# A gated linear attention and two dense blocks on one core: state products in four quarters of the array, y in two banks

## The chip, the cores and the metric

The kernel runs on one core of a Trainium2 chip. The metric is the device time of one execution in microseconds (us); the time before is the median of three runs, 859.57 us (857.78 to 859.61). The engines are TensorE (PE, with its weight loads as PEld), VectorE (DVE), ScalarE (ACT), GpSimd (POOL) and SyncE (SP), which issues nearly all transfers.

## The reference

Three parts follow one another, all in float32.

```python
for t in range(S):                                   # B, H, S, D = 4, 8, 768, 48
    state = alpha[:, :, t, :, None] * state + einsum('bhd,bhe->bhde', k[:, :, t], v[:, :, t])
    y[:, :, t] = einsum('bhd,bhde->bhe', q[:, :, t], state)
x = y as (B * S, H * D)                              # 3072 tokens, 384 columns
h = x @ w_in; x = (max(h, 0) + alpha * min(h, 0)) @ w_out      # 384 -> 2048 -> 384
return ((x @ w1) * (x @ w2)) @ w3 @ w_out2                     # 384 -> 1024 -> 1024 -> 384
```

## The kernel before

The attention is computed in 24 chunks of 128 time steps, six to each of the four batches; chunk n belongs to batch n // 6. Within a chunk the gates are multiplied up along time by a scan on VectorE, so that the recurrence becomes a masked product of scores with v, plus q times the state that the chunk starts from. The eight heads are laid out as four pairs: pair p holds its two heads (hh = 0 and 1) in partitions 0 to 47 and 64 to 111 of the tiles of q and k, and v is padded to 64 columns for each head.

The function `chunk` (line 340) traces the TensorE work of one chunk in this order: `state` (line 277) computes the update of the state, eight products into the tile `Up`; `yout` (line 293) computes y; `scores` (line 261) computes the scores of the next chunk into two tiles `scp`. `yout` has two stages that add into one PSUM bank `yp` of 128 x 512: eight products of v with the masked scores (`yp<-sc,v`), and eight of the state with q (`yp<-qt,sst`). A chunk that begins a batch (n % 6 == 0, `alone`) has no second stage. Head hh of pair p writes partitions 64 hh to 64 hh + 63 and column block p of the bank. So in the first stage the two heads of a pair use all 128 rows of the array and either its left or its right 64 columns; in the second stage head 0 uses rows 0 to 63 and columns 0 to 63, head 1 rows 64 to 127 and columns 64 to 127. The trace shows every one of these float32 products as two records, so a stage of eight products is 16 records of TensorE and 16 weight loads.

After its products, y is copied from the bank by ScalarE (line 310 for chunks 2 and 3, line 315 for the others; the helper `copy` is line 72), and `place` (line 321) moves it one tick later into the operand tile of the first dense block by six transfers for each copied piece, whole pairs 0 to 2 first and then pair 3 in four pieces (`PIECES`) that fill the remaining 32 partitions of each of the three column groups. The rows of `w_in` are put in the same order on the host.

The dense blocks work on 512 tokens at a time (T = 0 to 5), with `w_in` and `w_out` in high and low parts (`three`). `G1(T, f)` (line 377) makes nine products into a bank of 128 x 512 of the pool `pab` (tag `h`, two buffers that are taken in turn); ScalarE reads it (`u`, line 384) and then VectorE (`g`, line 386), after which the bank is free. `G2(T, f)` (line 391) makes nine products into three accumulators of the pool `pacc`, whose other three banks, by the parity w of T, are used by `Up`, `yp`, `scp` and `kTp` of the attention (`bank`, line 107). The eight PSUM banks are these six and the two of `pab`. The main loop goes through the pairs (T, f); each turn traces G1, some units of the attention, G2 of two turns earlier, and some units again (`attend`, line 465). Within a chunk the products made by `mm` (line 236) are pinned to their traced order on TensorE; elsewhere a planner orders the instructions of PE, DVE, ACT and POOL by costs of its own, and SP keeps the traced order.

In the opening (lines 407 to 446) four chunks run before any dense product, with dense products of a tile of zeros (`warm_up`, line 426) in between that also take the banks of `pab` in turn. After the attention, from about 430 us, TensorE works on the dense blocks alone. A fallback for gates outside a range of values (line 635 on) is in the program and isn't run on these inputs.

Of the kernel before, what the change touches and what calls it, by code (L numbers as in the profile page):

```python
# [9 lines left out]
F32 = mybir.dt.float32  # L10
# [11 lines left out]
B, H, S, D = 4, 8, 768, 48  # L22
DM, DFF, DF2 = 384, 2048, 1024
NT = B * S
CH = 128
NC_B = S // CH
NSTEP = B * NC_B
NP = H // 2
KD = DM // 128
DP = 64  # L30
# [19 lines left out]
def pieces():  # L50
    out, j = [], 0
    while j < 2 * D:
        (hh, e), (k, i) = divmod(j, D), divmod(j, EXT)
        n = min(D - e, EXT - i)
        out.append((k, 2 * D + i, hh, e, n))
        j += n
    return out


PIECES = pieces()  # L60
# [3 lines left out]
def fused_kernel(ctx, tc, qk, al, vv, wf, ws, m_alpha, ident, maskn, out):  # L64
# [3 lines left out]
    def f32(ap):  # L68
        return ap.bitcast(F32)

    def copy(out, in_):
        act.activation(out=out, in_=in_, func=AF.Copy)  # L72
# [7 lines left out]
    pab = ctx.enter_context(tc.tile_pool(name="pab", bufs=2, space=PSUM))  # L80
# [26 lines left out]
    def bank(shape, name, which):  # L107
        i = turn[which]
        turn[which] = (i + 1) % KD
        return pacc.tile(shape, F32, tag=f"acc{i}_{which}", name=name)  # L110
# [7 lines left out]
    sst = [ap1.tile([128, NP, DP], F32, name=f"sst{i}") for i in range(2)]  # L118
# [4 lines left out]
    def later(k, fn):  # L123
        due.setdefault(clock[0] + k, []).append(fn)
# [111 lines left out]
    def mm(*a, **k):  # L236
        ins = pe.matmul(*a, **k)  # L237
        if tight[0]:
            tc.keep_in_program_order(ins)
        tight[0] = True  # L240
# [34 lines left out]
    pairs = [(p, hh, slice(64 * hh, 64 * hh + DP)) for p in range(NP) for hh in range(2)]  # L275
# [17 lines left out]
    def yout(n, w):  # L293
        qt, v = st.pop(("qt", n)), st.pop(("v", n))
        sc = [st.pop(("sc", n, hh)) for hh in range(2)]
        alone = n % NC_B == 0
        ps = bank([128, NP, CH], "yp", w)
        for p, hh, r in pairs:
            mm(ps[r, p], v[:, 2 * p + hh], sc[hh][:, p], start=p == 0, stop=alone and p == NP - 1,
                      skip_group_check=True)  # L300
        if not alone:
            for p, hh, r in pairs:
                mm(ps[r, p], sst[n % 2][r, p], qt[r, p], start=False, stop=p == NP - 1, skip_group_check=True)
        T, c = divmod(n, SPT)
        if c == 0:
            new_x(T)
        single = n in (2, 3)
        if single:
            y = gp.tile([128, NP, CH], F32, tag="x1", name="yT1", bufs=KD)
            copy(y, ps)  # L310
        else:
            if c % 2 == 0:
                st["yT"] = ap2.tile([128, NP, 2, CH], F32, tag="yT", name="yT", bufs=1)
            y = st["yT"]
            copy(y[:, :, c % 2], ps)
            if c % 2 == 0:
                return
            y = y.rearrange("p a c t -> p a (c t)")
        x = f32(xt[T][:, 1, :, (c if single else c - 1) * CH:(c + 1) * CH])

        def place():
            q = (sp, act) if n == SPT - 1 else (sp, sp)
            for hh in range(2):
                q[hh].dma_start(out=x[hh * D:(hh + 1) * D], in_=y[64 * hh:64 * hh + D, :KD])
            for i, (k, to, hh, e, n_) in enumerate(PIECES):
                q[i % 2].dma_start(out=x[to:to + n_, k], in_=y[64 * hh + e:64 * hh + e + n_, KD])

        later(1, place)
# [3 lines left out]
    def new_x(T):  # L332
        xt[T] = xp.tile([128, 2, KD, TA], F32R, tag="x", name="x")
# [6 lines left out]
    def chunk(n, w, more=True):  # L340
        untie()
        state(n, w)
        yout(n, w)
        if more:
            scores(n + 1, w)
        load_v(n + 3)
# [60 lines left out]
    with tc.manual_schedule(engines={mybir.EngineType.SP}):  # L407
# [65 lines left out]
        for g in range(NG + LAG):  # L473
# [47 lines left out]
            if g in spans:  # L521
                U, steps = spans[g]
                pend = attn_units(U)
                tot, used, half = len(pend), 0, 0
# [22 lines left out]
        for i in range(NJ):  # L547
            t = w3_s[i]
            ps = bank([128, DM], "w34", 0)
# [86 lines left out]
    with tc.If(bad > 0):  # L636
        with tc.tile_pool(name="fa", bufs=1) as fa:
            S_ = fa.tile([128, NP, D], F32, name="S_")
            blk = fa.tile([128, 2], F32, name="blk")
            dve.memset(blk, 0.0)  # L640
            for hh in range(2):
                dve.memset(blk[64 * hh:64 * hh + 64, hh:hh + 1], 1.0)
            with tc.For_i(0, B, 1) as b:
                dve.memset(S_, 0.0)
                with tc.For_i(0, NC_B, 1) as c:
                    one = (bass.ds(b, 1), bass.ds(c, 1))
                    at = fa.tile([128, NP, CH], F32, name="at")
                    qt = fa.tile([128, 2, NP, CH], F32, name="qt")
                    vt = fa.tile([128, H, DP], F32, name="vt")
                    sp.dma_start(out=at, in_=al[one].rearrange("b c p a t -> p (b c a) t"))  # L650
                    sp.dma_start(out=qt, in_=qk[one].rearrange("b c p i a t -> p (b c i) a t"))
                    sp.dma_start(out=vt, in_=vv[one].rearrange("b c s h e -> s (b c h) e"))
                    for g in range(CH // TG):
                        yt = fa.tile([2, TG, NP, D], F32, name="yt")
                        for i in range(TG):
                            t = g * TG + i

                            def col(ap):
                                return ap[:, :, t:t + 1].to_broadcast([128, NP, D])

                            sel = fa.tile([128, 128], F32, name="sel")
                            dve.tensor_copy(out=sel, in_=idn[:, t:t + 1].to_broadcast([128, 128]))
                            vb = pacc.tile([128, NP, 2, D], F32, tag="acc0_0", name="vb")
                            pe.matmul(vb.rearrange("p a i e -> p (a i) e"), sel, vt[:, :, :D], start=True, stop=True)
                            kv = fa.tile([128, NP, D], F32, name="kv")
                            for hh in range(2):
                                r = slice(64 * hh, 64 * hh + 64)
                                dve.tensor_tensor(out=kv[r], in0=vb[r, :, hh],
                                                  in1=qt[r, 1, :, t:t + 1].to_broadcast([64, NP, D]), op=ALU.mult)
                            dve.tensor_tensor(out=S_, in0=S_, in1=col(at), op=ALU.mult)  # L670
                            dve.tensor_tensor(out=S_, in0=S_, in1=kv, op=ALU.add)
                            z = fa.tile([128, NP, D], F32, name="z")
                            dve.tensor_tensor(out=z, in0=S_, in1=col(qt[:, 0]), op=ALU.mult)
                            yp = pacc.tile([2, NP * D], F32, tag="acc1_0", name="yp")
                            pe.matmul(yp, blk, z.rearrange("p a e -> p (a e)"), start=True, stop=True)
                            copy(yt[:, i].rearrange("p a e -> p (a e)"), yp)
                        dst = y_d[one][:, :, g * TG:(g + 1) * TG]
                        whole = [(k, hh * D, hh, 0, D, k) for k in range(KD) for hh in range(2)]
                        for k, to, hh, e, n_, a in whole + [piece + (KD,) for piece in PIECES]:
                            sp.dma_start(out=dst[:, :, :, k, to:to + n_].rearrange("b c t e -> (b c) t e"),  # L680
                                         in_=yt[hh:hh + 1, :, a, e:e + n_])

        with tc.tile_pool(name="fb", bufs=1) as fb:
            wi = fb.tile([128, NF, KD, 128], F32, name="wi")
# [5 lines left out]
            for f in range(NF):  # L690
                for o, dst in enumerate((wi[:, f].rearrange("p k f -> p (k f)"), wo[:, f])):
                    t = fb.tile([128, DM, 2], I32, name="rw")
                    sp.dma_start(out=t.bitcast(I16).rearrange("p n c -> p (n c)")[:, :4 * DM - 1],
                                 in_=wf[f, :, o].bitcast(I16)[:, 1:])
                    upper(zf, t)
                    assemble(dst.bitcast(I32), zf, t)
            with tc.For_i(0, NTA, 1) as T:
                x = fb.tile([128, KD, TA], F32, name="xf")
                yv = y_d.rearrange("b c t k e -> (b c t) (k e)")
                for c in range(SPT):  # L700
                    yr = fb.tile([128, DM], F32, name="yr")
                    sp.dma_start(out=yr, in_=yv[bass.ds(T * TA + c * CH, CH)])
                    for k in range(KD):
                        ps = bank([128, 128], "tp", 1)
# [3 lines left out]
                for f in range(NF):  # L708
                    ps = pab.tile([128, TA], F32, tag="h", name="h")
                    for k in range(KD):  # L710
                        pe.matmul(ps, wi[:, f, k], x[:, k], start=k == 0, stop=k == KD - 1)
                    g = gp.tile([128, TA], F32, tag="g", name="g")
# [10 lines left out]
        with tc.tile_pool(name="fx", bufs=2) as fx:  # L723
            with tc.For_i(0, NTA, 1) as T:
                y = fx.tile([128, KD, TA], F32, name="x1")
                sp.dma_start(out=y, in_=x1_d[bass.ds(T, 1)].rearrange("b p k t -> p (b k) t"))
                e = xp.tile([128, 2, KD, TA], F32R, tag="x", name="x")
# [52 lines left out]
```

## Time and profile before

| | |
|---|---|
| median of three runs | 859.57 us (857.78 to 859.61) |
| the profiled execution | 856.45 us, span 854.7 us |
| PE busy | 834.7 us, 98% of the span, 4772 records |
| PEld busy | 686.0 us, 80% |
| DVE busy | 459.5 us, 54% |
| ACT busy | 352.6 us, 41% |
| POOL busy | 11.1 us, 1% |
| state products `yp<-qt,sst`, whole span | 320 records, 21.8 us busy, mean 275 ns |
| products with the scores `yp<-sc,v`, whole span | 384 records, 25.4 us busy, mean 275 ns |

The span runs from the first to the last recorded instruction of the profiled execution; its own time is 1.75 us longer. Busy time of an engine counts overlapping instructions once. A record of a TensorE product lasts longer than the step to the next one, since the products go through the array one behind the other and their ends are modelled. A merged row of the timeline reaches from the first start to the last end. L237 is the line of the helper `mm`, so the stages of a chunk are told apart by their tiles.

### The profile page before, as it was taken

What the parts mean: (1) busy time and instruction counts of PE and PEld (TensorE: products, weight loads), DVE (VectorE), ACT (ScalarE), POOL (GpSimd) and SP (SyncE); (2) the same over time, 40 slices, a digit from 0 to 9 for tenths busy, and PEclk for the clock granted to TensorE, in tenths of its full rate; (3) what the DMA queues carried; (4) which work ended last, traced back from release to release, by engine and by line L of the source; (5) the groups of instructions that cost most, each with busy time, mean ns of one, the idle gap of its engine ahead of it and who ended that gap; (6) DMA issues with size and microseconds to landing.
All of it is one profiled execution on the core that took longest, in us unless ns stands there. A gap on an engine that the chain in (4) does not pass through costs nothing.

```text
span 854.7 us, 11911 instructions
## 1 busy us (share of the span) xinstructions
PE 834.7 (98%) x4772; PEld 686.0 (80%) x4776; DVE 459.5 (54%) x643; ACT 352.6 (41%) x538; POOL 11.1 (1%) x53
## 2 busy tenths in 40 slices
PE   7899999999999999999999999999999999999996
PEld 4577888888888888888888889988888888888884
DVE  7899876665685586656335634552434435322221
ACT  3567665434454545454335534522223232221221
POOL 0000000000000000000000000000000000000000
PEclk9999999999999999999999999999999999999998
DMA  7667572321673385525003306420302203010001
GB/s 279 221 202 248 181 257 97 105 79 39 227 254 106 129 297 184 184 108 196 3 18 111 123 1 224 141 79 1 134 14 74 74 25 124 1 38 1 37 1 41
DMA packets 49104, 99.56 MB, mean 116 GB/s; under 512 B 4880, under 2 KB 25488, under 8 KB 49040
## 3 DMA queue, kind: packets, MB, share of 16 engines
q1 hardware_dynamic: 48800, 98.62, 34.0%
q8 instruction: 39, 0.64, 0.3%
q14 instruction: 25, 0.20, 0.1%
q10 hardware_dynamic: 240, 0.10, 0.0%
HBM read 75.63 MB, written 18.35 MB: 110 GB/s over the span
## 4 chain that ended last, share of the span: by engine, by line
PE 91%; DVE 4%; ACT 2%; issue 1%; DMA 1%; ACTq 0%; DVEq 0%; SPq 0%
PE ab L372 23%; PE h L372 21%; PE acc L372 11%; PE acc L397 8%; PE acc L398 7%; PE acc L400 7%; PE yp L237 4%; PE w L372 4%; PE scp L237 2%; PE Up L237 1%; PE kTp L256 1%; DMA al<-in_al_dram 1%; DVE al L214 1%; DVE w L151 1%; DVE sc L272 1%
## 5 line engine op out<-in xcount | busy, mean ns | idle before, releaser
L372 PE MATMUL h<-x,w 128*128 128x512 f32 x864 | 213.8, 391 | 3.5 <-ACT x L72 3.0
L372 PE MATMUL ab<-x,w 128*128 128x512 f32 x864 | 203.6, 389 | 0.0
L372 PEld LDWEIGHTS h<-x,w 128*128 128x128 f32 x864 | 161.3, 188 | 37.9 <-ACT x L72 3.5
L372 PEld LDWEIGHTS ab<-x,w 128*128 128x128 f32 x864 | 162.1, 188 | 33.6
L397 PE MATMUL acc<-gs,w 128*128 128x512 f32 x288 | 115.4, 401 | 0.0
L398 PE MATMUL acc<-gs,w 128*128 128x512 f32 x288 | 113.1, 393 | 0.0
L576 DVE TENSOR_TENSOR c<-ab,a 128x512 f32<-128x512 f32 x48 | 33.1, 690 | 145.3 <-PE ab L372 145.3
L384 ACT ACTIVATE u<-h,sgn 128x512 f32<-128x512 f32 x96 | 65.5, 682 | 108.0 <-PE h L372 107.8
L386 DVE SCALAR_TENSOR_TENSOR g<-h,salpha,u 128x512 f32<-128x512 f32 x96 | 71.7, 747 | 68.1 <-ACT u L384 67.7
L372 PE MATMUL acc<-cs,w 128*128 128x512 f32 x432 | 105.8, 389 | 0.0
L389 DVE SCALAR_TENSOR_TENSOR gs<-g,sgn,gs 128x512 fp32r<-128x512 f32 x96 | 71.9, 749 | 51.1 <-ACT gs L388 51.0
L372 PEld LDWEIGHTS acc<-cs,w 128*128 128x128 f32 x432 | 81.0, 188 | 17.2 <-DVE cs L579 0.4
L388 ACT ACTIVATE gs<-g,sgn 128x512 fp32r<-128x512 f32 x96 | 69.1, 719 | 54.0 <-DVE g L386 54.0
L400 PE MATMUL acc<-gs,w 128*128 128x512 f32 x288 | 81.4, 391 | 0.0
L72 ACT ACTIVATE a<-ab 128x512 f32<-128x512 f32 x48 | 28.8, 599 | 109.9 <-PE ab L372 109.9
L72 ACT ACTIVATE cs<-c 128x512 fp32r<-128x512 f32 x48 | 30.2, 629 | 93.4 <-DVE c L576 93.4
L397 PEld LDWEIGHTS acc<-gs,w 128*128 128x128 f32 x288 | 54.4, 189 | 12.4 <-issue 0.2
L400 PEld LDWEIGHTS acc<-gs,w 128*128 128x128 f32 x288 | 54.5, 189 | 11.6
L398 PEld LDWEIGHTS acc<-gs,w 128*128 128x128 f32 x288 | 54.5, 189 | 10.7
L72 ACT ACTIVATE top<-raw 128x768 f16<-128x768 bf16 (+1 forms) x39 | 41.8, 1071 | 29.6 <-DMA raw<-in_ws_dram 20.8
L579 DVE TENSOR_TENSOR cs<-c,cs 128x512 fp32r<-128x512 f32 x48 | 33.2, 691 | 30.8 <-ACT cs L72 30.8
L146 DVE SCALAR_TENSOR_TENSOR y<-raw,top 128x768 int32<-128x768 int32 (+1 forms) x39 | 36.9, 947 | 7.1 <-DMA ws_d<-y 4.5
(64 smaller groups left out, 656.9 us busy)
## 6 DMA issues: line engine op xcount, KB each, us to landing
raw<-in_ws_dram SPq DMA_DIRECT2D x22, 767.8 KB, 5.1
qk<-in_qk_dram SPq DMA_DIRECT2D x24, 512.0 KB, 5.7
raw<-in_wf_dram SPq DMA_DIRECT2D x16, 767.8 KB, 4.7
ws_d<-y SPq DMA_DIRECT2D x22, 384.0 KB, 3.0
al<-in_al_dram SPq DMA_DIRECT2D x24, 256.0 KB, 4.8
v<-in_vv_dram SPq DMA_DIRECT2D x24, 256.0 KB, 4.0
alx<-in_al_dram SPq DMA_DIRECT2D x8, 768.0 KB, 4.7
x_d<-x1e SPq DMA_DIRECT2D x18, 256.0 KB, 4.3
```

The lines of the kernel that those rows point to most:

```text
L72: act.activation(out=out, in_=in_, func=AF.Copy)
L146: return dve.scalar_tensor_tensor(out=y, in0=t[:, :, 0], scalar=13, in1=z[:, :n], op0=ALU.logical_shift_right, op1=ALU.bitwise_or)
L237: ins = pe.matmul(*a, **k)
L372: pe.matmul(ps, w, x, start=first and i == 0, stop=last and i == n - 1)
L384: act.activation(out=u, in_=ps, func=AF.Identity, scale=sg)
L386: dve.scalar_tensor_tensor(out=gt, in0=ps, scalar=sa, in1=u, op0=ALU.mult, op1=ALU.max)
L388: act.activation(out=s[:, 0], in_=gt, func=AF.Identity, scale=sg)
L389: dve.scalar_tensor_tensor(out=s[:, 1], in0=gt, scalar=sg, in1=f32(s[:, 0]), op0=ALU.mult, op1=ALU.subtract)
L397: pe.matmul(acc[T][m], r_out[f][:, 0, c], s[:, 0], start=f == 0, stop=False)
L398: pe.matmul(acc[T][m], r_out[f][:, 1, c], s[:, 0], start=False, stop=False)
L400: pe.matmul(acc[T][m], r_out[f][:, 0, c], s[:, 1], start=False, stop=f == NF - 1)
L579: dve.tensor_tensor(out=s[:, 1], in0=c, in1=f32(s[:, 0]), op=ALU.subtract)
```

## The change

`yout` takes two banks where it took one: a tile of 128 x 256 in the bank of `pacc` that it used before, and one of 128 x 256 in a bank of `pab`, under the tag `h` of the first dense product. Bank hh holds the heads hh of all four pairs. Pair p = 2 i + a of either head goes to partitions 64 a to 64 a + 63 and column block i. In the first stage the four products of head 0 come first and then those of head 1, alternating between left and right columns. In the second stage the four combinations of (row half hh, column half a) follow one another in the order (0, 0), (1, 1), (0, 1), (1, 0), once for i = 0 and once for i = 1. The copy of y becomes two copies of 128 x 256. The copied tile has the same shape as before, but another order of heads, which the rows of `w_in` on the host and the transfers of the fallback follow; `place` is unchanged.

```diff
-        ps = bank([128, NP, CH], "yp", w)
-        for p, hh, r in pairs:
-            mm(ps[r, p], v[:, 2 * p + hh], sc[hh][:, p], start=p == 0, stop=alone and p == NP - 1,
-                      skip_group_check=True)
+        ps = [bank([128, NP // 2, CH], "yp", w), pab.tile([128, NP // 2, CH], F32, tag="h", name="yp")]
+        half = [slice(64 * a, 64 * a + DP) for a in range(2)]
+        for hh in range(2):
+            for i in range(NP // 2):
+                for a in range(2):
+                    p = 2 * i + a
+                    mm(ps[hh][half[a], i], v[:, 2 * p + hh], sc[hh][:, p], start=i == 0, stop=alone and i == NP // 2 - 1,
+                       skip_group_check=True)
         if not alone:
-            for p, hh, r in pairs:
-                mm(ps[r, p], sst[n % 2][r, p], qt[r, p], start=False, stop=p == NP - 1, skip_group_check=True)
+            for i in range(NP // 2):
+                for hh, a in ((0, 0), (1, 1), (0, 1), (1, 0)):
+                    mm(ps[hh][half[a], i], sst[n % 2][half[hh], 2 * i + a], qt[half[hh], 2 * i + a], start=False,
+                       stop=i == NP // 2 - 1, skip_group_check=True)
...
-            copy(y, ps)
+            for hh in range(2):
+                copy(y[:, 2 * hh:2 * hh + 2], ps[hh])
...
-            copy(y[:, :, c % 2], ps)
+            for hh in range(2):
+                copy(y[:, 2 * hh:2 * hh + 2, c % 2], ps[hh])
...
-    order[:, :2 * D] = np.arange(KD * 2 * D).reshape(KD, 2 * D)
-    for k_, to, hh, e, n in PIECES:
-        order[k_, to:to + n] = KD * 2 * D + hh * D + e + np.arange(n)
+    head = [[4 * (g % 2) + 2 * a + g // 2 for a in range(2)] for g in range(NP)]
+    for k_ in range(KD):
+        for a in range(2):
+            order[k_, a * D:(a + 1) * D] = head[k_][a] * D + np.arange(D)
+    for k_, to, a, e, n in PIECES:
+        order[k_, to:to + n] = head[KD][a] * D + e + np.arange(n)
```

## Rows read from the trace of the kernel before

**Rows 1.** The profile's page, part 4: the chain of work that ended last, as shares of the span, first by engine and then by engine, operation and line.

```profile
PE 91%; DVE 4%; ACT 2%; issue 1%; DMA 1%; ACTq 0%; DVEq 0%; SPq 0%
PE ab L372 23%; PE h L372 21%; PE acc L372 11%; PE acc L397 8%; PE acc L398 7%; PE acc L400 7%; PE yp L237 4%; PE w L372 4%; PE scp L237 2%; PE Up L237 1%; PE kTp L256 1%; DMA al<-in_al_dram 1%; DVE al L214 1%; DVE w L151 1%; DVE sc L272 1%
```

**Rows 2.** Busy time of each engine in two long stretches (the first line names the columns: start and end of the stretch, its length, then busy time and instructions of each engine, the granted TensorE clock, the DMA engines' busy share, GB/s).

```profile
core 0: us, PE busy (x) PEld busy (x) DVE busy (x) ACT busy (x) POOL busy (x), PEclk, DMA share, GB/s
36.00:97.70 61.70, 55.98 (x393) 43.99 (x390) 58.14 (x80) 42.39 (x61) 3.29 (x10) 0.97 0.62 212
97.70:846.00 748.30, 748.30 (x4072) 622.41 (x4070) 372.99 (x516) 294.29 (x455) 5.26 (x29) 1.00 0.30 102
```

**Rows 3.** Timeline of TensorE in the opening, the two score products before which it stood still (start, length of the merged row, engine, line, operation, out<-in, form, count; in brackets the idle time before it and what ended it).

```profile
51.77 1.16 PE L237 MATMUL scp<-qt,kn 48*128 48x128 f32 x14 [0.59 <-DVE tmp L290]
...
82.64 1.16 PE L237 MATMUL scp<-qt,kn 48*128 48x128 f32 x14 [1.32 <-DVE sst L287]
```

**Rows 4.** Busy time of each engine in four stretches of the opening, columns as in rows 2.

```profile
41.00:55.00 14.00, 12.61 (x111) 9.80 (x112) 13.55 (x21) 9.39 (x14) 0.57 (x2) 1.00 0.78 275
55.00:78.00 23.00, 23.00 (x138) 18.86 (x137) 22.37 (x31) 15.40 (x22) 1.11 (x3) 1.00 0.60 202
...
80.90:82.65 1.75, 0.43 (x5) 0.24 (x4) 1.75 (x4) 1.75 (x4) 0.00 (x0) 1.00 0.90 309
...
83.85:87.25 3.40, 3.40 (x9) 2.63 (x10) 3.40 (x6) 1.92 (x3) 0.00 (x0) 0.50 1.00 377
```

**Rows 5.** Timeline of all engines from 20 to 45 us, columns as in rows 3; SPq is the instruction queue of SyncE.

```profile
21.54 1.39 SPq L324 DMA_DIRECT2D x<-yT  x2
...
23.18 0.58 ACT L72 ACTIVATE kT<-kTp 128x512 f32<-128x512 f32 x1
...
23.81 0.69 PE L237 MATMUL Up<-v,kT 128*64 128x64 f32 x16
...
41.00 1.65 PE L372 MATMUL h<-x,w 128*128 128x512 f32 x6 [3.01 <-ACT x L72]
```

**Rows 6.** Groups of TensorE products by line and operation from 97 to 430 us: out<-in, form, count | busy time in us, mean ns of one | idle time before them in us.

```profile
L237 PE MATMUL yp<-sc,v 128*64 128x128 f32 x271 | 18.0, 274 | 0.0
L237 PE MATMUL yp<-qt,sst 64*64 64x128 f32 x240 | 16.4, 275 | 0.0
```

**Rows 7.** Timeline of one chunk of the attention, 241.2 to 245.6 us, TensorE's products (PE) and weight loads (PEld), columns as in rows 3.

```profile
241.29 0.69 PE L237 MATMUL Up<-v,kT 128*64 128x64 f32 x16
...
241.75 0.86 PEld L237 LDWEIGHTS yp<-sc,v 128*64 128x64 f32 x16
241.81 1.05 PE L237 MATMUL yp<-sc,v 128*64 128x128 f32 x16
...
242.78 0.85 PEld L237 LDWEIGHTS yp<-qt,sst 64*64 64x64 f32 x16 [0.17 <-issue]
242.78 1.09 PE L237 MATMUL yp<-qt,sst 64*64 64x128 f32 x16
...
243.80 1.16 PE L237 MATMUL scp<-qt,kn 48*128 48x128 f32 x16
```

**Rows 8.** The state products of that chunk, TensorE alone, in three short looks that end at 242.93, 243.04 and 243.15 us; each row merges the products that had started by then.

```profile
242.78 0.33 PE L237 MATMUL yp<-qt,sst 64*64 64x128 f32 x2
...
242.78 0.44 PE L237 MATMUL yp<-qt,sst 64*64 64x128 f32 x4
...
242.78 0.55 PE L237 MATMUL yp<-qt,sst 64*64 64x128 f32 x6
```

**Rows 9.** Groups of ScalarE copies by form over the whole span: out<-in, form, count | busy time in us, mean ns of one | idle time before them and what ended it.

```profile
L72 ACT ACTIVATE yT<-yp 128x512 f32<-128x512 f32 x24 | 14.1, 587 | 11.4 <-PE yp L237 11.2
...
L72 ACT ACTIVATE w<-w3y 128x512 fp32r<-128x512 f32 x16 | 9.3, 623 | 1.9 <-DMA w3y<-ws_d 1.9
...
L72 ACT ACTIVATE wo_s<-wo 128x384 fp32r<-128x384 f32 x8 | 3.9, 518 | 1.2 <-DMA wo<-ws_d 1.2
```

**Rows 10.** Timeline from 238 to 249 us: around the chunk of rows 7, the vector operation that is the last to read a bank of the first dense product, the copy of y, and the next first dense product.

```profile
239.33 0.74 DVE L386 SCALAR_TENSOR_TENSOR g<-h,salpha,u 128x512 f32<-128x512 f32 x1
...
242.99 0.74 DVE L386 SCALAR_TENSOR_TENSOR g<-h,salpha,u 128x512 f32<-128x512 f32 x1
...
244.60 0.58 ACT L72 ACTIVATE yT<-yp 128x512 f32<-128x512 f32 x1
...
247.07 2.21 PE L372 MATMUL h<-x,w 128*128 128x512 f32 x9
```

**Rows 11.** Timeline from 301.3 to 307.0 us: a first dense product, the vector operation that is the last to read its bank, and the next first dense product.

```profile
301.32 1.42 PE L372 MATMUL h<-x,w 128*128 128x512 f32 x5
...
304.10 0.74 DVE L386 SCALAR_TENSOR_TENSOR g<-h,salpha,u 128x512 f32<-128x512 f32 x1
...
304.63 2.20 PE L372 MATMUL h<-x,w 128*128 128x512 f32 x9
```

More of the change, by code (lines that the diff above doesn't have):

```diff
@@ L677, in fused_kernel @@
                         dst = y_d[one][:, :, g * TG:(g + 1) * TG]
-                        whole = [(k, hh * D, hh, 0, D, k) for k in range(KD) for hh in range(2)]
-                        for k, to, hh, e, n_, a in whole + [piece + (KD,) for piece in PIECES]:
+                        whole = [(k, a * D, a, 0, D, k) for k in range(KD) for a in range(2)]
+                        for k, to, a, e, n_, g_ in whole + [piece + (KD,) for piece in PIECES]:
+                            hh, pr = g_ // 2, 2 * (g_ % 2) + a
                             sp.dma_start(out=dst[:, :, :, k, to:to + n_].rearrange("b c t e -> (b c) t e"),
-                                         in_=yt[hh:hh + 1, :, a, e:e + n_])
+                                         in_=yt[hh:hh + 1, :, pr, e:e + n_])
         with tc.tile_pool(name="fb", bufs=1) as fb:
```

## The prediction

> **What bounds the kernel now.** I read the chain of waits first. TensorE holds 91% of it, and the products of y (`yp`) hold 4% of the span [rows 1]: the part that the change touches is on the path, and it is small. Next comes the table of busy time by stretch, because a share of the span says nothing about where a saved microsecond stays saved. From 97.7 to 846 us TensorE is busy in 748.30 of 748.30 us, with VectorE at 373 and ScalarE at 294 [rows 2]. There, whatever TensorE need not do shortens the run. From 36 to 97.7 us TensorE has 5.7 us of gaps while VectorE is busy in 58.1 of 61.7 us [rows 2]. Its two longest stops in front of score products end with VectorE, 0.59 us at 51.8 and 1.32 us at 82.6 [rows 3], and around them VectorE has 13.55 of 14.00 and 22.37 of 23.00 us [rows 4]. Before 82.6 us, then, a faster TensorE mostly waits longer for VectorE. The opening before 41 us is bounded in another way: the transfers of y into x begin on SP's queue at 21.54 us, and the first dense product starts at 41.00, after 3.01 us in which TensorE waited for x [rows 5].
>
> The list by line and form, limited to 97 to 430 us, says how much of the changed work lies in the safe stretch: 240 records of state products, none with idle time before it [rows 6]. At 16 records a chunk that is 15 chunks. The other five chunks with a state stage (n = 1 to 5) lie before 82.6 us.
>
> **The state products.** One chunk's timeline shows the stage alone: 16 records from 242.78 on, 1.09 us from first start to last end, and the scores at 243.80, so the stage costs 1.02 us of TensorE's time [rows 7]. Three short looks show its inside: two records have started by 242.93, four by 243.04, six by 243.15, and the merged row grows from 0.33 to 0.44 to 0.55 us [rows 8]. So two products, the two heads of a pair, run abreast, each further pair of records costs 0.11 us, and 0.33 + 7 x 0.11 = 1.10 us, the 1.09 of the row. After the change four combinations of row half and column half follow one another. If four run abreast, there are four steps in place of eight: 0.33 + 3 x 0.11 + about 0.01 for the later start of the third and fourth = 0.67 us. The gain is 1.09 - 0.67 = 0.42 us a chunk.
>
> No row of before shows four abreast, so I bound it. Each half of it is shown: column halves abreast on the same rows (`yp<-sc,v`, 16 records in 1.05 us, the same 0.11 us step) and row halves abreast into two banks (`scp`, 16 in 1.16 us) [rows 7]. Issue could be the limit: the state update `Up` starts its 16 records between 241.29 and 241.81 us [rows 7], 0.033 us each, so four take at most 0.13 us; with that step the stage is 0.35 + 3 x 0.13 = 0.74 us and the gain 0.35. The lower end is a four that runs as two pairs, gain 0, or worse (the second rival). I take 0.42, because the rows of both halves are the nearest and both have room: 15 x 0.42 = 6.3 us, and 15 x 0.35 = 5.3 us at the issue bound.
>
> A rule of the Trainium skill speaks against this. First the row: the 16 weight loads of `yp<-sc,v` all use the 128 rows that the products in flight use, and they still begin before the products and end 0.25 us before them (241.75 + 0.86 = 242.61 against 242.86) [rows 7]. The page "TensorE: Matmul & The Clock Gate", section "Part 3: Packing small matmuls — row/col tiling", says that a weight load goes beside a product in flight only if the two are in different groups of rows. By it the third and fourth product of a four could not load under the first two, and the result would be the second rival below. The trace disagrees with the rule, which is why that rival gets little.
>
> **The products with the scores.** Still eight, alternating left and right columns, 16 records at 0.11 us: no change. Their order is now by head, so the first four need only head 0's masked scores; from 97 us on nothing waited there [rows 6], so that is worth nothing. The flags that begin and end the sums cost nothing either: they ride on products that are there anyway. The rows of `w_in` are put in order on the host, the transfers of y are the same in number and size, and the edited fallback isn't run.
>
> **The copies.** One copy of 128 x 512 (587 ns) becomes two of 128 x 256. No row has that width on ScalarE. The bounds are 0.29 us (half of 587) and 0.52 (the 384-wide one). 512 to 384 columns goes from 623 to 518 ns [rows 9], so 256 columns take some 0.41 from SBUF and 0.37 from PSUM, by 0.036 less. Two make 0.74, which is 0.15 us more than now, between 0 and 0.45; 24 chunks give 3.6 us of ScalarE, hidden since it is busy in 39% of the long stretch [rows 2]. Where that cover is gone, in the opening, it delays the transfers by those 0.15 us.
>
> **The bank of the dense product.** This is the added wait. The pool has two banks in turn. A chunk's second half of y now takes the one that is next, so it waits for the last reader of the dense product before the last, and the dense product after the chunk takes the bank of the one just before the chunk. Behind the waiting product stand the rest of the chunk, the second dense products and everything after, since TensorE takes them in order. In the usual place both waits are over: the older reader ends at 240.07, before y begins at 241.81; the younger ends at 243.73 and the next dense product starts at 247.07; and the copy of y ends at 245.18, far ahead of the dense product after that [rows 7, 10]. It gets tight where the planner has put the chunk elsewhere, in the middle of a dense product: that product ends at 302.74, its reader at 304.84, and the next one starts at 304.63 [rows 11]. If that one needs the same bank, it is 0.2 to 0.3 us late. I count two such places (one for each of two T), 0.5 us, with bounds 0 and 24 x 0.25 = 6.0 us.
>
> **The opening.** Chunks 1 to 3 lose 0.42 us each on TensorE. For chunk 1 the next `Up` at 23.81 follows ScalarE's copy of `kT`, 23.18 + 0.58 [rows 5], not TensorE, so nothing comes of it there. What it does give is an earlier start of SP's transfers at 21.54: 0.42 less the 0.15 of the longer copy. I take 0.3 us, with 0 to 0.8 as bounds. Chunks 4 and 5 stand before the two waits for VectorE [rows 3]: 0, at most 0.84.
>
> **Sum.** 6.3 - 0.5 + 0.3 = 6.1 us. The profiled execution took 856.45 us, 1.75 more than its span, so it would take 850.35. It lies 3.12 us below the median of 859.57; taken off the median, the forecast is 853.5 us.
>
> **Rivals.**
>
> *The fours run as pairs, or the bank eats the gain.* The second pair waits until the first has streamed, and the step stays at 0.11 us for two. Gain 0, with at most 0.5 us for the bank: 859.6 to 860.1. For it: no row of before has more than two abreast. Against: both halves of the combination are there at full rate [rows 7]. The same time comes out if all 24 chunks meet the wait of rows 11: -6.3 + 6.0 = -0.3 us.
>
> *Slower: the second pair's weights lie bare.* Third and fourth product share rows with the first and second; if their load can't go under those, each pair pays it. Its price is in the first step of the stage: two records are all that started between 242.78 and 242.93 [rows 8], so this step is at least 0.15 us against 0.11, some 0.05 bare. Eight steps of 0.16 in place of 0.11 make the stage 0.4 us longer, 15 x 0.4 = 6.0: 865.6 us. It decides as soon as a step that finds its rows in use takes more than 0.11 us. Against it: `yp<-sc,v` loads under its own rows [rows 7].
>
> *The opening turns.* After 1.75 us in which TensorE was busy only 0.43, the granted clock stood at 0.50, its 1.2 GHz level, for 3.4 us [rows 4]; half of these are lost, 1.7 us. Shorter state products leave TensorE emptier in front of x (3.01 us idle already [rows 5]). One or two more such drops: 853.5 + 1.7 to 3.4 = 855.2 to 856.9. The other way, all five early chunks count (2.1 us in place of 0.3) and today's drop goes (1.7): 853.5 - 1.8 - 1.7 = 850.0.
>
> *The change does not do what it says*: the planner could tear the fours apart. I give it no time of its own: the products of a chunk are pinned to their traced order.
>
> **How the numbers follow.** The forecast, 853.5 with its own range 852 to 855.5 (the issue bound and the bank's places), gets 0.58; the opening turning against it 0.12; for it 0.07; pairs or bank 0.12; bare weights and the like 0.11. A measurement of this kernel tells about 0.2%, 1.7 us, from no change, that is 857.8 to 861.3. Faster: 0.58 + 0.12 + 0.07 = 0.77. Same: 0.12. Slower: 0.11. The range reaches from all early chunks with the drop gone and no wait for the bank (850.0 - 0.5 = 849.5) to the case without gain (859.8).
>
> **What would show it.** Right: in the stretch after 97 us the 16 state records of a chunk take about 0.67 us from first start to last end and the scores follow 0.60 us after the first; a short look finds four records started within 0.05 us; no dense product idles in front for more than 0.3 us; two copies of about 0.37 us each. Wrong: 16 records still in 1.09 us (pairs), or over 1.3 us (bare weights); idle time before first dense products that ends with VectorE or the copy of y (the bank); a second stretch at a granted clock of 0.50.

## The result and the profile after

The changed kernel takes 865.23 us (median of seven runs, 859.25 to 868.57), the kernel before 858.77 us in its seven runs: a ratio of 1.0069, 95% interval 1.005 to 1.0089. It is slower by 0.7%, where 853.5 us was forecast; the range ended at 859.8. The profiled execution took 860.56 us, 4.1 more than the one of before, with a span of 858.8 us. Lines of the code from 317 on have moved down by 8 (`h` is L380, `u` L392, `g` L394).

The page of the changed kernel, busy time and the chain of waits:

```profile
PE 832.2 (97%) x4772; PEld 680.5 (79%) x4776; DVE 458.6 (53%) x643; ACT 353.1 (41%) x562; POOL 13.4 (2%) x53
...
PE 81%; DVE 6%; DMA 4%; ACT 3%; issue 2%; SPq 0%; ACTq 0%; DVEq 0%
```

TensorE had less to do and held 81% of the chain instead of 91% [rows 1]. VectorE, transfers and ScalarE hold more of it. Where that happened shows in the stretches (columns as in rows 2):

```profile
36.00:97.70 61.70, 56.17 (x381) 43.88 (x380) 58.24 (x81) 42.39 (x64) 4.39 (x10) 0.94 0.62 211
97.70:849.70 752.00, 746.50 (x4084) 618.30 (x4080) 371.36 (x515) 294.35 (x472) 5.49 (x29) 1.00 0.30 102
42.79:46.20 3.41, 3.41 (x12) 2.28 (x12) 2.98 (x4) 1.63 (x3) 0.57 (x2) 0.50 1.01 402
83.75:87.16 3.41, 3.41 (x17) 2.80 (x16) 3.41 (x6) 2.49 (x3) 0.00 (x0) 0.50 0.99 353
230.52:233.93 3.41, 3.41 (x14) 2.70 (x11) 3.41 (x5) 2.31 (x4) 0.66 (x2) 0.50 0.42 113
```

The long stretch, which had no gap at all [rows 2], now has 752.00 - 746.50 = 5.5 us of them. And there are three stretches of 3.4 us at a granted clock of 0.50 (the 1.2 GHz level) where before had one [rows 4]; at half the clock TensorE loses half of such a stretch, 1.7 us. What TensorE stood still for, by line from 97 to 430 us (columns as in rows 6):

```profile
L237 PE MATMUL scp<-qt,kn 48*128 48x128 f32 x256 | 20.6, 288 | 3.3 <-DVE tmp L290 1.9 <-ACT x1e L72 1.4
L237 PE MATMUL yp<-sc,v 128*64 128x128 f32 x272 | 18.6, 275 | 2.2 <-DVE g L394 2.2
L237 PE MATMUL yp<-qt,sst 64*64 64x128 f32 x240 | 10.0, 282 | 0.0
```

The state products fell from 16.4 to 10.0 us busy, as meant. The 5.5 us stand in the other two rows: products with the scores wait for `g`, the last reader of a bank of the dense product, and score products for `tmp` (VectorE's read of `Up`) and `x1e` (a copy by ScalarE out of an accumulator). Now the waits in full, at the start of a block of tokens. First the kernel before, TensorE's timeline there (columns as in rows 3):

```profile
215.32 1.07 PE L372 MATMUL h<-x,w 128*128 128x512 f32 x4
216.32 0.69 PE L237 MATMUL Up<-v,kT 128*64 128x64 f32 x16
216.83 1.06 PE L237 MATMUL yp<-sc,v 128*64 128x128 f32 x16
217.82 1.16 PE L237 MATMUL scp<-qt,kn 48*128 48x128 f32 x16
...
219.33 1.40 PE L372 MATMUL h<-x,w 128*128 128x512 f32 x5
```

The chunk stands in the middle of a dense product, four of its nine records ahead and five behind. In the changed kernel, all engines, the same place and the next block:

```profile
213.97 0.69 PE L237 MATMUL Up<-v,kT 128*64 128x64 f32 x16
...
216.55 2.35 PE L380 MATMUL h<-x,w 128*128 128x512 f32 x9
...
219.09 2.31 PE L380 MATMUL h<-x,w 128*128 128x512 f32 x9
...
224.01 1.09 ACT L72 ACTIVATE top<-raw 128x768 f16<-128x768 bf16 x1 [0.46 <-DMA raw<-in_ws_dram]
...
224.97 0.66 ACT L392 ACTIVATE u<-h,sgn 128x512 f32<-128x512 f32 x1
...
226.46 0.66 PE L237 MATMUL yp<-sc,v 128*64 128x128 f32 x8 [0.21 <-DVE g L394]
...
229.40 0.41 DVE L290 TENSOR_TENSOR tmp<-sst,Up 128x256 f32<-128x256 f32 x1
...
229.86 1.51 PE L237 MATMUL scp<-qt,kn 48*128 48x128 f32 x14 [1.73 <-DVE tmp L290]
...
308.58 1.08 ACT L72 ACTIVATE top<-raw 128x768 f16<-128x768 bf16 x1 [3.71 <-DMA raw<-in_ws_dram]
...
310.13 0.67 ACT L392 ACTIVATE u<-h,sgn 128x512 f32<-128x512 f32 x1
...
310.92 0.74 DVE L394 SCALAR_TENSOR_TENSOR g<-h,salpha,u 128x512 f32<-128x512 f32 x1
...
311.72 0.55 PE L237 MATMUL yp<-sc,v 128*64 128x128 f32 x6 [1.38 <-DVE g L394]
```

The half of a dense product that stood ahead of the chunk is gone, and two whole ones come behind it, at 216.55 and 219.09. The second ends at 221.40, but its reader `u` starts only at 224.97. On ScalarE `top`, a step in the decoding of the raw weights, stands ahead of `u`, and it begins when the raw weights are there, at 224.01. So `g`, which follows `u`, is late, and the next chunk's second half of y, which needs that bank, stops TensorE for 0.21 us. Then the scores stop it for 1.73 us: their second tile takes the bank of `Up`, which `tmp` reads at 229.40. VectorE's order has changed there too: `tmp` comes behind `y`, which needs `top` (227.87), and behind a `g` (228.74), while in the kernel before `tmp` (225.49) came ahead of that `y` (229.26). The clock falls 0.7 us after that stop. In the next block the same chain is plainer: `top` waits 3.71 us for its transfer, `u` and `g` follow, and y stands 1.38 us.

### The profile page after: what moved, and what is told of

Read it like the earlier page. It is cut to its first block, busy times and chain, and to the rows that moved or that the text cites. A ratio compares the mean times of both kernels' runs of the same rounds, so it can differ in the third digit from the quotient of the medians.

```text
span 858.8 us, 11917 instructions
## 1 busy us (share of the span) xinstructions
PE 832.2 (97%) x4772; PEld 680.5 (79%) x4776; DVE 458.6 (53%) x643; ACT 353.1 (41%) x562; POOL 13.4 (2%) x53
## 4 chain that ended last, share of the span: by engine, by line
PE 81%; DVE 6%; DMA 4%; ACT 3%; issue 2%; SPq 0%; ACTq 0%; DVEq 0%
PE ab L380 23%; PE h L380 17%; PE acc L380 11%; PE acc L405 7%; PE acc L406 6%; PE acc L408 6%; PE w L380 4%; DMA raw<-in_ws_dram 3%; PE yp L237 2%; PE scp L237 2%; DVE y L146 1%; DVE g L394 1%; PE Up L237 1%; DVE w L151 1%; DMA raw<-in_wf_dram 1%
## 5 line engine op out<-in xcount | busy, mean ns | idle before, releaser
L380 PE MATMUL h<-x,w 128*128 128x512 f32 x864 | 215.1, 393 | 0.0
L380 PE MATMUL ab<-x,w 128*128 128x512 f32 x864 | 203.7, 389 | 0.0
L380 PEld LDWEIGHTS h<-x,w 128*128 128x128 f32 x864 | 162.0, 189 | 34.7 <-DVE g L394 0.3
L380 PEld LDWEIGHTS ab<-x,w 128*128 128x128 f32 x864 | 162.1, 188 | 33.6
L392 ACT ACTIVATE u<-h,sgn 128x512 f32<-128x512 f32 x96 | 65.4, 681 | 105.6 <-PE h L380 105.3
L380 PE MATMUL acc<-cs,w 128*128 128x512 f32 x432 | 105.8, 389 | 0.0
L394 DVE SCALAR_TENSOR_TENSOR g<-h,salpha,u 128x512 f32<-128x512 f32 x96 | 71.7, 747 | 58.8 <-ACT u L392 58.7
L380 PEld LDWEIGHTS acc<-cs,w 128*128 128x128 f32 x432 | 81.0, 188 | 17.2 <-DVE cs L587 0.4
L72 ACT ACTIVATE top<-raw 128x768 f16<-128x768 bf16 (+1 forms) x39 | 41.7, 1069 | 30.6 <-DMA raw<-in_ws_dram 21.8
```

Of the source, the lines that this page charges most:

```text
L380: pe.matmul(ps, w, x, start=first and i == 0, stop=last and i == n - 1)
L392: act.activation(out=u, in_=ps, func=AF.Identity, scale=sg)
L394: dve.scalar_tensor_tensor(out=gt, in0=ps, scalar=sa, in1=u, op0=ALU.mult, op1=ALU.max)
```

## The experiments

The expectations go by these theories. A: the second half of y in the banks of the dense products spoils the order of TensorE, in the opening and at the starts of blocks. B: the fours themselves cost. C: the copies cost. D: another bank at the block starts would leave the loss where it is. All ratios are to the kernel before, timed beside each experiment on the same chip; experiments e1 to e4, e5 to e8 and e9 to e11 ran on three different chips.

**e1_banks**, the two banks without the fours: pairs 0 and 1 in one bank, 2 and 3 in the other, and the old pairs of state products (shown against the changed kernel; the first stage and the copies follow the same split).

```diff
...
-            for i in range(NP // 2):
-                for hh, a in ((0, 0), (1, 1), (0, 1), (1, 0)):
-                    mm(ps[hh][half[a], i], sst[n % 2][half[hh], 2 * i + a], qt[half[hh], 2 * i + a], start=False,
-                       stop=i == NP // 2 - 1, skip_group_check=True)
+            for p, hh, r in pairs:
+                mm(ps[p // 2][r, p % 2], sst[n % 2][r, p], qt[r, p], start=False, stop=p % 2 == 1, skip_group_check=True)
...
```

> Bank split alone: y in two banks (pairs 0 and 1 in the old one, pairs 2 and 3 in the bank of the dense product), two copies, but the eight state products in their old pairs, two abreast. Theory A (the turn of the dense product's banks puts the planner's order out at the block starts and in the opening; TensorE idles and its clock falls): all of the loss without the gain, that is 865.2 plus the 6.3 to 8.4 us that the fours save, 871 to 874 us, with the same places of idle time as in the changed kernel. Theory B (the four products abreast themselves upset something, the clock say): no loss without them, 858 to 860 us.

Measured: 864.69 us, ratio 1.0054 (1.0035 to 1.0073). The loss is there without the fours, so B falls. TensorE's order is that of the changed kernel at both places: the scores of chunk 4 stand ahead of the first dense product (after a stop of 3.99 us, at 41.95), and no half of a dense product stands ahead of the chunk at 214.61. A's number was too high: it asked for 6 to 8 us more than the changed kernel, and none came. So in this order the fours bring no gain that these times show; which waits take it was not split, and the waits for `g` are shorter here (0.3 us from 97 to 430 us, against 2.2).

**e2_copies**, before's single bank, read by two copies of 128 x 256.

```diff
-            copy(y[:, :, c % 2], ps)
+            for i in range(2):
+                copy(y[:, 2 * i:2 * i + 2, c % 2], ps[:, 2 * i:2 * i + 2])
...
```

> Two copies alone: y in one bank and in the old pairs, copied by two copies of 128x256. Theory A: the same as before within 0.2%, 857 to 860.5 us, since the order on TensorE is that of before. Theory C (the longer copying delays the transfers of y and what hangs on them): slower by 3 us or more, 862 to 866.

Measured: 859.32 us, ratio 0.9998 (0.9983 to 1.0013). C falls.

**e3_first**, the changed kernel, with both halves of y of the first chunk traced in a block (n = 12, 16, 20) in the attention's own banks. TensorE's order at the starts of blocks is then that of before (at 214.15 us again four records of a dense product ahead of the chunk and five behind it).

```diff
-        ps = [bank([128, NP // 2, CH], "yp", w), pab.tile([128, NP // 2, CH], F32, tag="h", name="yp")]
+        shape = [128, NP // 2, CH]
+        ps = [bank(shape, "yp", w)]
+        ps += [bank(shape, "yp", w) if n % SPT == 0 and n > 2 * SPT else pab.tile(shape, F32, tag="h", name="yp")]
```

> The changed kernel, but in the first chunk of the last three blocks (n = 12, 16, 20) the second half of y takes the attention's own third bank and not one of the dense product. Theory A: dense products go ahead of that chunk again, the idle time near 226, 310 and 392 us (4.1 us) and the drop of the clock near 230 us go, the opening stays as it is: 855 to 860 us. Theory D (what costs is the wait for the bank itself on TensorE, in whatever order): the other 20 chunks still wait, 862 to 866.

Measured: 859.45 us, ratio 1.0004 (0.9985 to 1.0022). A's range holds it and D falls: the other chunks still use the shared banks. Its groups from 97 to 430 us have no more idle time in front of y:

```profile
L237 PE MATMUL scp<-qt,kn 48*128 48x128 f32 x256 | 21.0, 287 | 2.1 <-ACT x1e L72 1.0 <-DVE tmp L290 0.8 <-DVE sst L287 0.3
L237 PE MATMUL yp<-sc,v 128*64 128x128 f32 x266 | 17.8, 275 | 0.0
```

**e6_pin_alone**, the other place alone: in the changed kernel the opening's order put back, block starts as changed.

```diff
-            pe.transpose(ps[:, p], kn[:, p], idn)
+            tr = pe.transpose(ps[:, p], kn[:, p], idn)
+            if n == SPT:
+                tc.keep_in_program_order(tr)
...
-            u += [lambda: (untie(), scores(n0, w), kT(n0, w)), lambda: prep(n0 + 1)]
+            u += [lambda: (scores(n0, w), kT(n0, w)), lambda: prep(n0 + 1)]
```

> The changed kernel with the opening alone put back (the scores and the transpose of chunk 4 stay behind the first dense product), the block starts as changed. By theory A the loss of some 10 us has two places, the opening (one dropped clock of 3.4 us, worth 1.7 us, and the order of chunks 4 and 5) and the three block starts (4 us of idle TensorE and a dropped clock of 1.7 us): it lies between the two kernels, 859 to 862 us, and TensorE still stops at the three block starts. Rival F (the opening alone made e4 fast): 854 to 856 us. Rival G (the opening is worth nothing): 864 to 866 us.

Measured: 859.01 us, ratio 1.0003 (0.998 to 1.0025), at the lower end of what A said; F and G fall. What was left at the block starts is still there:

```profile
L237 PE MATMUL scp<-qt,kn 48*128 48x128 f32 x256 | 20.2, 286 | 2.6 <-DVE tmp L292 1.9 <-ACT x1e L72 0.7
L237 PE MATMUL yp<-sc,v 128*64 128x128 f32 x272 | 18.6, 275 | 1.9 <-DVE g L396 1.8
```

**e4_first_pin** and **e9_best_again**, one kernel with both edits (e3 and e6), timed on two chips.

> As e3_first, and the scores and transposes of chunk 4 pinned behind the first dense product, as the order of before had them. Theory A: the clock keeps its level in the opening too, and what is left is the gain of the fours, 6.3 us less some 1.5 us for the first chunks' third bank: 852 to 856 us. If the opening's order is nothing: the time of e3_first.

> The kernel of e4 again, now beside that of e5 on one chip in one call. If its gain is real: ratio to before 0.992 to 0.996 as in e4, about 854 to 856.5 us.

Measured: 854.93 us, ratio 0.9937 (0.992 to 0.9955), and 855.63 us, ratio 0.997 (0.995 to 0.999). This version beats both kernels. Taken alone, e3 takes 0.0065 off the changed kernel's 1.0069 and e6 0.0066; both together would make 0.9938. e4 came out there; e9 gained 0.0032 less. That the two places simply add up is likely, but no closer shown than that.

**e5_pairs_good** and **e10_pairs_again**, the kernel of e4 with the old pairs of e1. TensorE's order is that of e4.

> The kernel of e4 (TensorE in the order of before) with the old pairs of state products and the bank split by pairs of heads; both halves of y have the same two banks as in e4, and TensorE's order is that of e4. Theory A (the fours are worth their 8.3 us of TensorE wherever its order is kept; what the changed kernel lost, it lost by its order): 861 to 863.5 us, 6 to 8 us over e4. Rival E (most of e4's lead over the kernel before comes from the opening and the bank, and the fours' gain is waited away on other engines): 855 to 858 us.

> The kernel of e5 again (old pairs of state products in the good order). Theory A: the fours are worth 5 to 8 us in this order, so this is 5 to 8 us over e9 and within 0.3% of before. Rival E (the fours' gain is waited away): within 2 us of e9.

Measured: 858.97 us, ratio 1.0002 (0.9984 to 1.002), and 858.93 us, ratio 1.0003 (0.9986 to 1.002). Between e4 and e5, on two chips, the fours are worth 0.0065 of the time, 5.6 us; between e9 and e10, on one chip, 3.3 us. That lies between A and E: in the good order some 40 to 67% of the 8.4 us that the state products lose (21.8 to 13.3 or 13.4) reaches the end. The groups over the whole span, e10 first, then e9:

```profile
L237 PE MATMUL scp<-qt,kn 48*128 48x128 f32 x384 | 30.1, 286 | 4.6 <-DVE sst L289 1.4 <-DVE kn L232 1.4 <-ACT x1e L72 1.3
...
L237 PE MATMUL yp<-qt,sst 64*64 64x128 f32 x320 | 21.8, 275 | 0.0
```

```profile
L237 PE MATMUL scp<-qt,kn 48*128 48x128 f32 x384 | 31.8, 287 | 4.8 <-DVE sst L289 1.7 <-DVE tmp L292 1.6 <-DVE kn L232 0.8
...
L237 PE MATMUL yp<-qt,sst 64*64 64x128 f32 x320 | 13.3, 282 | 0.0
```

With the fours a wait for `tmp` appears (1.6 us), and the score products are busy 1.7 us longer. One such place in e9, all engines, and then TensorE and `tmp` at the same chunk in e10:

```profile
238.66 0.95 DVE L146 SCALAR_TENSOR_TENSOR y<-raw,top 128x768 int32<-128x768 int32 x1
...
240.20 1.23 DVE L214 TENSOR_TENSOR_SCAN al<-al,scan 128x516 f32<-128x516 f32 x1
...
241.34 0.40 DVE L292 TENSOR_TENSOR tmp<-sst,Up 128x256 f32<-128x256 f32 x1
...
241.79 1.04 PE L237 MATMUL scp<-qt,kn 48*128 48x128 f32 x13 [1.04 <-DVE tmp L292]
```

```profile
244.45 0.40 DVE L292 TENSOR_TENSOR tmp<-sst,Up 128x256 f32<-128x256 f32 x1
...
245.08 1.16 PE L237 MATMUL scp<-qt,kn 48*128 48x128 f32 x16
```

The second score tile takes the bank of `Up`. In e9 TensorE begins this chunk 4.39 us sooner than in e10 (`Up` at 238.18 and 242.57) and its scores, with the shorter stage, 4.81 us sooner (240.27 and 245.08), but VectorE, which does `y` and `al` first, reads `Up` only 3.11 us sooner (241.34 and 244.45). So the wait is not the 0.42 us of the stage alone: TensorE has gained on VectorE from chunk to chunk and meets it here. It wasn't tried to give `Up` another bank, so how much of the missing half this wait is stays open.

**e8_raw_pool**, the changed kernel with the copy `top` on GpSimd instead of ScalarE.

```diff
-        copy(z[:, :n].bitcast(F16).rearrange("p (n c) -> p n c", c=2)[:, :, 1], t.bitcast(BF16)[:, :, 2])
+        pool.tensor_copy(out=z[:, :n].bitcast(F16).rearrange("p (n c) -> p n c", c=2)[:, :, 1], in_=t.bitcast(BF16)[:, :, 2])
```

> The changed kernel, with one copy of the weights' decoding (line 142) moved from ScalarE to GpSimd, so that ScalarE no longer stands behind the raw weights' transfer (lines 216, 301 and 382 us of the chain) while u, g and with them the bank of y are due. Theory H (that wait is why the bank comes late at the block starts): the stops of 0.2 to 1.7 us there go, the time falls by 3 to 5 us to 860 to 862 us. Theory A (the order by itself puts the dense products behind the chunk, whatever frees the bank): stops of 0.5 us or more remain at the block starts, 863.5 to 866 us.

Measured: 865.21 us, ratio 1.0082 (1.0051 to 1.0112). By its time H falls; by its mechanism it doesn't. From 97 to 430 us nothing waits for `g` any more, though no half of a dense product stands ahead of the chunk (at 223.73) here either. So it was `top` ahead of `u` on ScalarE that made the bank late. The edit brought costs of its own elsewhere:

```profile
L237 PE MATMUL scp<-qt,kn 48*128 48x128 f32 x256 | 20.2, 286 | 3.6 <-ACT x1e L72 2.2 <-DVE sst L287 1.3
L237 PE MATMUL yp<-sc,v 128*64 128x128 f32 x256 | 16.8, 274 | 0.0
```

```profile
43.48 0.80 PE L237 MATMUL scp<-qt,kn 48*128 48x128 f32 x4 [5.12 <-DVE kn L232]
```

The first stop of the opening grew from 3.99 to 5.12 us, and 2.2 us wait for `x1e`. As a test of the price of the raw transfer it is spoilt by these; as one of where the wait comes from it stands.

**e7_open_bank**, the kernel of e4 with the second half of y of chunks 0 to 3 in the attention's banks too.

```diff
-        ps += [bank(shape, "yp", w) if n % SPT == 0 and n > 2 * SPT else pab.tile(shape, F32, tag="h", name="yp")]
+        ps += [bank(shape, "yp", w) if n < SPT or n % SPT == 0 and n > 2 * SPT else pab.tile(shape, F32, tag="h", name="yp")]
```

> The kernel of e4, and chunks 0 to 3 of the opening also take the bank of the second half of y from the attention's own buffers. In e4 the warm-up products waited 1.49 us at 32 us of the span for the copy of such a half. If that stop is on the path: 853 to 854.5 us, and the stop is gone. Rival: the opening ends on the vector engine and on the transfers, not on this bank, and the time stays that of e4, 854.5 to 856 us.

Measured: 855.93 us, ratio 0.9974 (0.9955 to 0.9993), the rival's range. The stop of 1.49 us was a matter of that one execution: in e9, the same kernel, it is 0.22.

**e11_more_warm**, the kernel of e4 with ten more warm-up products at the end of the opening.

```diff
-WARM0, WARM, REST = 18, 2, 18
+WARM0, WARM, REST = 18, 2, 28
```

> The kernel of e4 with 28 warm-up products of zeros in place of 18 at the end of the opening, which fill most of the stop of 2.76 us ahead of the first dense product (10 more at 0.22 us). If a stop of this length is what the granted clock falls after, the mean granted clock of the timed runs rises against e9 (by 0.001 to 0.002) and the time falls by 1 to 2 us, 853 to 855 us; the end of the opening itself can't move, since ScalarE's copy of x sets it. Rival (the clock falls after later stops, or without regard to this one): the time and the mean clock of e9.

Measured: 856.21 us, ratio 0.9965 (0.994 to 0.999); the mean granted clock of the timed runs was 0.9943 against 0.9936 in e9. The expected gain of 1 to 2 us did not come. In its profile the stop ahead of the first dense product is down from 2.71 to 0.55 us, and the clock stays up behind it. e9 and then e11, TensorE's timeline:

```profile
40.25 3.91 PE L384 MATMUL h<-x,w 128*128 128x512 f32 x9 [2.71 <-ACT x L72]
```

```profile
41.46 1.66 PE L384 MATMUL h<-x,w 128*128 128x512 f32 x6 [0.55 <-ACT x L72]
```

and the granted clock there, 0.50 in e9 and 1.00 in e11 (columns as in rows 2):

```profile
40.44:43.85 3.41, 3.41 (x9) 2.48 (x8) 3.41 (x6) 2.90 (x4) 0.00 (x0) 0.50 0.60 209
```

```profile
40.44:43.85 3.41, 2.37 (x10) 1.29 (x8) 3.38 (x6) 2.67 (x5) 0.00 (x0) 1.00 0.83 287
```

The profile of e11 has one stretch at 0.50 all the same, at another place (14.7 to 18.1 us), where e9 has none, so both profiled executions have one in all. For the time it is inconclusive: an effect of 1 us can't be told at these intervals.

## Why the prediction was wrong

**The state products: right.** One chunk of the changed kernel, TensorE's timeline:

```profile
245.95 1.04 PE L237 MATMUL yp<-sc,v 128*64 128x128 f32 x16
246.93 0.67 PE L237 MATMUL yp<-qt,sst 64*64 64x128 f32 x16
247.52 1.16 PE L237 MATMUL scp<-qt,kn 48*128 48x128 f32 x16
```

and the state products in three short stretches that end at 247.02, 247.13 and 247.24 us, as in rows 8, and then the weight loads that have begun by 247.00:

```profile
246.93 0.34 PE L237 MATMUL yp<-qt,sst 64*64 64x128 f32 x4
...
246.93 0.45 PE L237 MATMUL yp<-qt,sst 64*64 64x128 f32 x8
...
246.93 0.56 PE L237 MATMUL yp<-qt,sst 64*64 64x128 f32 x12
...
246.92 0.21 PEld L237 LDWEIGHTS yp<-qt,sst 64*64 64x64 f32 x8 [0.17 <-issue]
```

Four records instead of two in the first stretch, and four more for each 0.11 us: 0.67 us, and the scores 0.59 us after the first. With that the rivals "run as pairs" and "weights lie bare" fall. The rule of the Trainium skill (page "TensorE: Matmul & The Clock Gate", section "Part 3: Packing small matmuls — row/col tiling"), by which a weight load overlaps only with products in other rows, is not what these rows show: eight loads, those of a whole four of products at two records each, have begun 0.08 us after the first, while only four records of products have begun, and no step grows by it. (The same section also speaks of loads into a background weight buffer, which that rule leaves out.) That the measured 865.23 lies beside the 865.6 of "weights lie bare" is chance.

**The copies: right.** 48 copies at a median of 375 ns, where 0.37 us was expected, and in e2 they cost nothing that its interval (0.9983 to 1.0013) can tell:

```profile
L72 ACT ACTIVATE yT<-yp x48: 362/375/386, 14.7 to 431.1; 128x256 f32<-128x256 f32 x48
```

**The bank of the dense product: wrong, and this decided.** The step priced the wait at 0.5 us, from the places that the kernel before had, and held TensorE's order for fixed. In the usual place there is indeed no wait: the chunk above has none. Nor did the idle time come where the prediction looked for it, before first dense products (0.0 us from 97 to 430 us). But a tile in the turn of the dense products' two banks also ties the order in which the planner may put them. The first chunk of a block is traced before the next dense products, and those could no longer go ahead of it. So the row 215.32 of before, half a dense product ahead of the chunk, was gone, its readers came later, and they met ScalarE's wait for raw weights. That wait is nothing new (3.35 us before the `top` at 226.41 in the kernel before), but there no product of y needed what stood behind it. The rival "does not do what it says" asked whether the planner would tear the fours apart, and gave it no time since a chunk's products are pinned. The pin held; what moved was everything that isn't pinned. e3 prices the block starts at 0.0065 of the time, 5.6 us, inside the bounds of 0 to 6.0 that the step gave; the sum took 0.5, and the upper bound stood in a rival alone.

**The opening: wrong in sign.** +0.3 us was taken. The planner put the scores of chunk 4 ahead of the first dense product:

```profile
41.76 0.48 PE L237 MATMUL scp<-qt,kn 48*128 48x128 f32 x2 [3.99 <-DVE kn L232]
...
42.17 3.71 PE L380 MATMUL h<-x,w 128*128 128x512 f32 x9
```

TensorE stood for 3.99 us instead of 3.01 [rows 5], and the clock fell for the next dense product. e6 prices this order at 0.0066 of the time, 5.7 us. What the price is made of stays open: in e6's own profile the clock falls after the first dense product's stop as well (0.50 from 41.26 to 44.67, after 2.70 us). Why the planner chose so was not traced; that it follows from the second bank is shown by e1, where the fours are absent and the order and the loss are there.

**"Whatever TensorE need not do shortens the run": half right.** In the good order 3.3 to 5.6 us of the 8.4 that the state products save come out (e9 and e10, e4 and e5). One cause is shown, that the scores run into VectorE's read of `Up`; its share is not. Rows 3 had that wait already, twice in the opening; the prediction asked what is late next only there.

**The clock** was a rival ("the opening turns", at most 2 drops and 856.9 us) and came in larger. By an estimate: the timed runs of the changed kernel list mean granted clocks of 0.980 to 0.992, on average 0.9866, and those of before beside e1 to e4 0.9934; 0.0068 of 859 us is 5.8 us, as much as most of the 6.5 us between the medians. The same working gives e1 only 1.7 of its 4.6 us (0.9914), so the clock is not the whole price of the order. A stop of TensorE thus costs its length and in some cases a stretch of low clock behind it. In the profiled execution -8.4 us of state products, +5.5 us of gaps in the long stretch and +3.4 us for two more drops make +0.5, where +4.1 was measured; the remaining 3.6 us were not split further; the opening and waits within merged rows are where they may lie. This execution, at a clock of 0.992, was the second fastest of the seven, so what the median run lost beyond it stands in no trace.

## What to carry to other kernels

When a tile moves into a pool that other work takes in turn, compare TensorE's order before and after, and not only the hardware wait for the bank: a turn ties everything that shares it to the order of tracing. Where an order matters, pin it, or keep the odd tile out of the shared turn at the few places where it is traced ahead of work that should overtake it; here that turned +0.7% into -0.3 to -0.6%. A stage made shorter on a full engine brings the next products forward, so look up who frees their banks before the gain is counted.

## What the runs showed of the hardware

Four float32 products on the four quarters of the array step at 0.11 us, the same as two did [rows 8]. In the profile of the changed kernel the granted clock fell to 0.50 for 3.41 us after three stops of TensorE (3.99 us to 41.76, 1.39 to 83.35, 1.73 to 229.86), each time 0.4 to 1.0 us after its end, and not after another of 1.38 us, to 311.72. The length of a stop alone did not decide it: in the kernel before the clock stayed up after 3.01 us and fell after 1.32 us [rows 3 to 5], and in one and the same kernel it fell after 2.71 us (e9) and stayed up after 2.76 us (e4, at 41.57). Moving the 39 copies `top` to GpSimd (e8) went with longer work on VectorE that nobody had touched. The operation `gs`, in the changed kernel and then with the move (minimum, median and maximum in ns, first and last start):

```profile
L397 DVE SCALAR_TENSOR_TENSOR gs<-g,sgn,gs x96: 721/752/755, 49.0 to 518.5; 128x512 fp32r<-128x512 f32 x96
```

```profile
L397 DVE SCALAR_TENSOR_TENSOR gs<-g,sgn,gs x96: 720/751/1540, 51.1 to 524.8; 128x512 fp32r<-128x512 f32 x96
```

The median stayed, but twelve of the 96 ran beside a `top` on GpSimd, and eight of these took 860 to 1540 ns (the longest from 132.64 us, the copy from 132.62); of the other 84 none took over 800. The copies have the same median on both engines (1072 ns on GpSimd, 1077 on ScalarE), but on GpSimd 12 of them took 1246 to 2981 ns, each beside work on VectorE. The Trainium skill (page "Perfetto Trace Analysis", section "Optimizing Scalar/DVE Operations") says that GpSimd and VectorE share a port, so that moving work between them might not help. The move here was from ScalarE, so only the shared port bears on it; that `gs` grew only where the two engines worked at once agrees with it, though no run here separates the port from other causes.
